# W_in brought in group by group to both halves, and x of the first blocks asked for sooner: a convolution and GELU layer on one Trainium2 core

## Chip, core and metric

The kernel runs on one core of a Trainium2 chip. The metric is the device time of one execution in microseconds (us). Before the change the median of three timed runs is 682.07 us (681.24 to 682.17). The profile is of one execution of 681.4 us; from its first to its last instruction it spans 679.6 us, and all times below are counted from that first instruction.

## What is computed

The input x has 8 sequences of 4,096 tokens with 192 channels. First comes a causal convolution over 7 tokens, whose weights are a softmax for each of 8 heads of 24 channels. Then comes a feed-forward layer with an exact GELU between two matrix products.

```python
w = softmax(weight, axis=-1)                          # 8 heads x 7 taps
x_pad = np.concatenate([np.zeros((B, 6, D)), x], axis=1)
conv = np.einsum('hk,bskhg->bshg', w, unfolded(x_pad)).reshape(B * S, D)
h = conv @ w_in                                       # 192 -> 2048
g = 0.5 * h * (1.0 + erf(h / sqrt(2)))
out = g @ w_out                                       # 2048 -> 192
```

## The kernel before

**Tiling.** The 32,768 tokens are cut into two halves of 16,384. The lower 64 partitions hold the first half, the upper 64 the second. The 192 channels are stored as 3 (`NP`) channels on each of 64 partitions, so a 64-row matmul tile of TensorE serves one half, and the two halves run on different rows of the array. A half is worked through in 35 blocks (`NB`, sizes `WS`): six of 256 tokens, then 29 of 512.

**Slots.** For each block, `mm1` (line 698) makes the 2,048 hidden columns in slots: 8 slots of 256 columns for a block of 256 tokens, 16 slots of 128 for one of 512. ScalarE applies the GELU to a slot's result (line 645), which goes into `gT`; two PSUM buffers `hp` alternate, so slot u waits for the GELU of slot u-2. Between the slots TensorE does shares of `mm2` (lines 742 and 777), the second product, for the block before. For blocks 0 and 1 the convolution is done on TensorE with diagonal weights (`pconv`, line 661); from block 2 on VectorE does it (`conv`, line 495), seven taps on the transposed x.

**W_in on chip.** Both halves need the whole of W_in, so `win` must hold it on partitions 0 to 63 and again on 64 to 127. HBM is read once: GpSimd issues four transfers (`win_in`, line 371), which turn float32 into bfloat16, each to one half of the partitions with two groups of 256 columns: groups 0 and 4 to the lower half, 1 and 5 to the upper, then 2 and 6 to the lower, 3 and 7 to the upper. VectorE copies each to the other half (`dup`, line 459). In its first slots each half uses the groups that came to it directly; the order is the table `CH` (line 86), of which group `ch // 2` and parity `ch % 2` are read in `mm1` and the rows of W_out in `mm2` and `mm2_t`. The first slot waits for two transfers, which share a semaphore, since the halves get theirs by different transfers.

**What sets the order at the start.** GpSimd issues, one after another: three W_in transfers, a part of the diagonal weights (line 397), the fourth, then four of W_out (line 404). SyncE issues x of block 0 and then waits twice: for the fourth small step of the softmax before block 1 (`S_PRO` 4, line 847), and for W_out's third transfer before blocks 2 and 3 (line 849). VectorE runs a list written out by hand (lines 542 to 553): transposes of block 0, its share of `conv_out`, copies of W_in, transposes of block 1, the last copy, `conv_out` of block 1, and then the plan of the blocks from 2. `cast` (line 221) makes the bfloat16 input of `pconv`, on ScalarE for block 0 and on GpSimd for block 1. `mm1` of the first block has its own waits:

```python
if (n, i) == (0, 0):
    t.wait_ge(S_WIN[0], 32)
if n == 0 and i in (4, 6):
    t.wait_ge(S_WIN[i // 2 - 1], 16)
if n == 0 and i in (2, 4, 6):
    t.wait_ge(S_DUPE, 1 + i // 2)
```

## Time and profile before

| what | profile before |
|---|---|
| span | 679.6 us |
| TensorE busy | 674.0 us, 99% |
| ScalarE busy | 537.1 us, 79% |
| VectorE busy | 526.2 us, 77% |
| GpSimd busy | 32.1 us, 5% |
| GELU (line 645), one of 512 | 1.02 us |
| copy within `win` (line 466), one of 4 | 0.56 us |
| W_in, issue to landing | 4.0, 5.5, 6.4 and 7.3 us |
| W_out, issue to landing | 7.1, 7.4, 7.6 and 7.9 us |

The busy time of an engine is the time in which it has an instruction under way. Matmul ends are modelled, so a busy TensorE isn't one at its peak. A row of the profile names a line, an engine, an operation and its tiles (output <- inputs); in square brackets stands how long the engine was idle before it and what ended that. PE is TensorE, PEld its weight loads, DVE VectorE, ACT ScalarE, POOL GpSimd and SP SyncE; a "q" after a name means the engine's own issuing of transfers. Everything that the change touches happens in the first 30 us; the remaining 650 us run in a steady rhythm.

### The profile page before, as it was taken

The page shows a single profiled execution, that of the slowest core. Times are in us where ns is not written, and L with a number is a line of the kernel's source. Part 1 is how long each engine was busy: PE and PEld are TensorE (multiplying, and loading weights), DVE is VectorE, ACT ScalarE, POOL GpSimd, SP SyncE. Part 2 cuts the span into 40 slices and gives each one's busy share as a digit, 9 for nine tenths or more (in the row PEclk, how much of TensorE's full clock was granted, in tenths as well). Part 3 has the DMA queues.
Part 4 walks back from the last instruction along what each step waited for, and adds up shares of the span by engine and source line. Part 5 has one row for each costly group of instructions (what it writes and reads, how often), then busy time and mean ns, then how long its engine had stood idle before and what let it go on. Part 6 is the DMA issues. An engine that isn't in the chain of part 4 may idle for free.

```text
span 679.6 us, 27115 instructions
## 1 busy us (share of the span) xinstructions
PE 674.0 (99%) x12632; PEld 412.8 (61%) x12632; DVE 526.2 (77%) x607; ACT 537.1 (79%) x550; POOL 32.1 (5%) x54
## 2 busy tenths in 40 slices
PE   8999999999999999999999999999999999999998
PEld 7899655555555555555555555555555555555557
DVE  5899978977779877789777798777797777887511
ACT  7899978777778877777877787777878777778772
POOL 5010000000000000000000000000000000000000
DMA  9435324224443234442244432344422344310123
GB/s 147 113 85 140 71 61 93 50 49 96 95 96 79 40 73 96 95 94 51 50 93 95 96 74 51 66 96 95 96 55 50 87 96 95 87 43 16 49 49 96
DMA packets 134145, 53.66 MB, mean 79 GB/s; under 512 B 127376, under 2 KB 134032, under 8 KB 134032
## 3 DMA queue, kind: packets, MB, share of 16 engines
q1 hardware_dynamic: 130224, 49.76, 32.7%
q0 software_dynamic: 2688, 1.57, 1.7%
q8 instruction: 99, 1.62, 1.0%
q10 hardware_dynamic: 1120, 0.59, 0.3%
q14 instruction: 14, 0.11, 0.1%
HBM read 28.31 MB, written 25.17 MB: 79 GB/s over the span
## 4 chain that ended last, share of the span: by engine, by line
PE 95%; DMA 2%; DVE 1%; POOL 0%; SPq 0%; issue 0%; ACT 0%; ACTq 0%
PE hp L732 47%; PE ob L793 43%; PE ob L764 5%; DMA wout<-in_moe_w_out_dram 1%; PE hp L764 1%; DVE acc L521 1%; DMA xin<-in_x_dram 0%; SPq L336 0%; POOL wout L405 0%; DMA wsb<-in_weight_dram 0%; DVE xT L493 0%; DVE wcol L454 0%; DVE xc L521 0%; POOL win L374 0%; POOL dg L397 0%
## 5 line engine op out<-in xcount | busy, mean ns | idle before, releaser
L645 ACT ACTIVATE gT<-hp 128x1024 bf16<-128x1024 f32 x512 | 523.2, 1024 | 128.6 <-PE hp L732 125.3
L732 PE MATMUL hp<-xc,win 64*64 64x512 bf16 (+3 forms) x6072 | 418.6, 365 | 1.8 <-DMA win<-in_moe_w_in_dram 1.1
L793 PE MATMUL ob<-gT,wout 64*64 64x512 bf16 x5376 | 366.3, 376 | 0.0
L521 DVE SCALAR_TENSOR_TENSOR acc<-xT,wcol,acc 128x1024 f32<-128x1024 f32 (+1 forms) x330 | 295.5, 948 | 2.4 <-ACT acc L618 2.4
L732 PEld LDWEIGHTS hp<-xc,win 64*64 64x64 bf16 (+1 forms) x6072 | 188.4, 106 | 134.8 <-ACT xc L200 1.3
L793 PEld LDWEIGHTS ob<-gT,wout 64*64 64x64 bf16 x5376 | 173.4, 118 | 121.8
L323 DVE STREAM_TRANSPOSE osb<-ob 128x512 f32<-128x512 f32 x84 | 74.0, 884 | 129.4 <-PE ob L793 129.4
L493 DVE STREAM_TRANSPOSE xT<-xin 128x1536 f32<-128x1536 f32 (+2 forms) x39 | 74.6, 1920 | 3.3 <-DMA xin<-in_x_dram 3.2
L521 DVE SCALAR_TENSOR_TENSOR xc<-xT,wcol,acc 128x1024 bf16<-128x1024 f32 (+1 forms) x66 | 60.4, 954 | 0.0
L764 PE MATMUL ob<-wout,gT 64*128 64x192 bf16 x896 | 47.5, 243 | 0.1
L423 POOL COPY xT<-xT 128x18 f32<-128x18 f32 x30 | 22.9, 763 | 514.1 <-DVE xT L493 491.9
L764 PEld LDWEIGHTS ob<-wout,gT 64*128 64x128 bf16 x896 | 38.5, 94 | 5.9 <-PE ob L764 0.6
L514 DVE TENSOR_SCALAR acc<-xT,wcol 128x512 f32<-128x512 f32 (+2 forms) x60 | 33.7, 604 | 1.1
L294 ACT ACTIVATE osb<-ob 128x192 f32<-128x192 f32 x2 | 0.7, 331 | 7.1 <-PE ob L764 7.1
L659 PE MATMUL hp<-const-bfloat16-1.0 128*128 128x128 bf16 x48 | 5.3, 310 | 0.8 <-PEq L873 0.8
L764 PE MATMUL hp<-wout,gT 64*128 64x192 bf16 x128 | 5.9, 243 | 0.0
L618 ACT ACTIVATE acc<-xT,wcol 128x256 f32<-128x256 f32 (+1 forms) x9 | 5.2, 580 | 0.5 <-DVE xT L493 0.5
L659 PEld LDWEIGHTS hp<-const-bfloat16-1.0 128*128 128x128 bf16 x48 | 5.0, 145 | 0.8 <-issue 0.8
L292 DVE COPY osb<-ob 128x192 f32<-128x192 f32 x2 | 0.7, 358 | 6.1 <-PE ob L764 6.1
L764 PEld LDWEIGHTS hp<-wout,gT 64*128 64x128 bf16 x128 | 5.3, 94 | 0.0
L279 ACT ACTIVATE osb<-ob 128x384 f32<-128x384 f32 x10 | 4.9, 489 | 0.0
L202 DVE CAST xc<-ob 64x256 bf16<-64x256 f32 (+3 forms) x8 | 2.9, 357 | 2.6 <-PE ob L677 2.4
(35 smaller groups left out, 28.8 us busy)
## 6 DMA issues: line engine op xcount, KB each, us to landing
out_dram<-osb SPq DMA_DIRECT2D x124, 192.0 KB, 3.2
xin<-in_x_dram SPq DMA_DIRECT2D x116, 192.0 KB, 4.0
xin<-in_x_dram SPq DMA_DIRECT2D x22, 96.0 KB, 2.5
win<-in_moe_w_in_dram POOLq DMA_DIRECT2D x4, 192.0 KB, 5.9
wout<-in_moe_w_out_dram POOLq DMA_DIRECT2D x4, 192.0 KB, 7.5
out_dram<-osb ACTq DMA_DIRECT2D x4, 96.0 KB, 1.9
out_dram<-osb SPq DMA_DIRECT2D x4, 96.0 KB, 2.5
xin<-in_x_dram ACTq DMA_DIRECT2D x2, 96.0 KB, 2.5
```

Of the source, the lines that this page charges most:

```text
L279: e.activation(out=dst, in_=src, func=AF.Copy).then_inc(S_EVA)
L323: v.transpose(ap(osb[m % 2], j, [[8 * C, 128], [C // 2, TB // 32], [NP, 32]]), bank(ring(m, j)),).then_inc(S_EV)
L423: g.tensor_copy(dst, src).then_inc(S_HALO)
L493: v.transpose(out, src).then_inc(S_TR)
L514: ins = v.tensor_scalar(a, src, wk, None, ALU.mult)
L521: ins = v.scalar_tensor_tensor(dst, src, wk, a, op0=ALU.mult, op1=ALU.add)
L618: a.activation(out=acc[n % 2][:, p * TB : p * TB + w], in_=ap(xT[n % 2], p * XW + HX, [[NP * XW, 128], [1, w]]), func=AF.Copy, scale=wcol[ ...
L645: a.activation(out=ap(gT[n % 2], i * c * 2 * w, dst), in_=ap(hp[u % 2], 0, src), func=AF.Gelu,).then_inc(S_GELU)
L659: t.matmul(hp[1][:, 0:128], one, one)
L732: ins = t.matmul(hp[u % 2][fo : fo + fw, o : o + w], ap(win, f1, [[NP * F, 64], [2, fw]]), xc[n % 2][r, p * TB : p * TB + w], start=(p == ...
L764: ins = t.matmul(bb[sub], gT[m % 2][r, c0 : c0 + 128], wout[r, CH[sub][i] * C : (CH[sub][i] + 1) * C], start=(ph == 0 and k == 0), stop=(p ...
L793: ins = t.matmul(bank(ring(m, j), slice(64 * h, 64 * h + 64), w), ap(wout, 64 * hf * NF * C + CH[h][i] * C + j, [[NF * C, 64], [NP, 64]],) ...
```

## The change

Each W_in transfer now brings the 256 columns of one group to the lower half and those of the neighbouring group to the upper half at once, in the place of the even group in both. So transfer q serves a slot of both halves by itself, and has a semaphore of its own. The order is groups 0 and 1, 4 and 5, 2 and 3, 6 and 7. `dup` makes two copies for each transfer, of half the size each, from either half into the odd group's place of the other. In the upper half neighbouring groups therefore lie exchanged, which `mm1` undoes with `^ hf`. The slots take own and copied groups in the order own 0, own 1, copied 0, copied 1, own 2, copied 2, own 3, copied 3. The copies come in another order on VectorE. SyncE asks for x of block 1 after the second step of the softmax instead of the fourth, for block 2 after the fourth W_in transfer instead of W_out's third, and for block 3 after W_out's fourth. `mm2` waits for W_out's third and fourth transfers together. The purpose is an earlier first slot and an earlier convolution of block 2.

```diff
-    CH = [
-        [4 * (i // 8) + 2 * ((i // 4 + hf * (i < 8)) % 2) + 8 * (i // 2 % 2) + i % 2 for i in range(NF)]
-        for hf in range(2)
-    ]
+    CG = [[0, 4, 1, 5, 2, 3, 6, 7], [1, 5, 0, 4, 3, 2, 7, 6]]
+    CH = [[2 * CG[hf][i // 2] + i % 2 for i in range(NF)] for hf in range(2)]
...
-        def part(s, hf):
-
-            return FQ * (2 * s + hf), [[NP * F, 64], [4 * FQ, 2 * NP], [1, FQ]]
+        def part(q):
+
+            return FQ * (4 * (q % 2) + 2 * (q // 2))
...
-            def win_in(s, sm, hfs):
-                for hf in hfs:
-                    c0, pat = part(s, hf)
-                    g.dma_start(
-                        ap(win, 64 * hf * NP * F + c0, pat), ap(wint, c0, pat)
-                    ).then_inc(sm[hf], 16)
+            def win_in(q):
+                g.dma_start(
+                    ap(win, part(q), [[NP * F, 128], [F, NP], [1, FQ]]),
+                    ap(wint, part(q), [[FQ, 2], [NP * F, 64], [F, NP], [1, FQ]]),
+                ).then_inc(S_WIN[q], 16)
...
-            def dup(s, hf):
-
-                if s == 0:
-                    v.wait_ge(S_WIN[0], 32)
-                else:
-                    v.wait_ge(S_WIN[1 + hf], 16)
-                c0, pat = part(s, hf)
-                v.tensor_copy(
-                    ap(win, 64 * (1 - hf) * NP * F + c0, pat), ap(win, 64 * hf * NP * F + c0, pat)
-                ).then_inc(S_DUPE)
+            def dup(q):
+
+                v.wait_ge(S_WIN[q], 16)
+                for hf in range(2):
+                    pat = [[NP * F, 64], [F, NP], [1, FQ]]
+                    v.tensor_copy(
+                        ap(win, 64 * (1 - hf) * NP * F + part(q) + FQ, pat),
+                        ap(win, 64 * hf * NP * F + part(q), pat),
+                    ).then_inc(S_DUPE)
...
-            dup(0, 0)
-            dup(0, 1)
-            dup(1, 0)
+            dup(0)
+            dup(1)
             for p in range(NP):
                 trans(1, p)
-            dup(1, 1)
+            dup(2)
+            dup(3)
...
-                if (n, i) == (0, 0):
-                    t.wait_ge(S_WIN[0], 32)
-                if n == 0 and i in (4, 6):
-                    t.wait_ge(S_WIN[i // 2 - 1], 16)
-                if n == 0 and i in (2, 4, 6):
-                    t.wait_ge(S_DUPE, 1 + i // 2)
+                if n == 0:
+                    j = (0, 1, 0, 1, 2, 2, 3, 3)[i]
+                    if i in (0, 1, 4, 6):
+                        t.wait_ge(S_WIN[j], 16)
+                    else:
+                        t.wait_ge(S_DUPE, 2 * j + 2)
...
-                        f0 = 256 * (ch // 2) + ch % 2
+                        f0 = FQ * ((ch // 2) ^ hf) + ch % 2
...
-                        if n < 2 and un[:2] == (0, 0) and un[2] in (0, 8, 12):
-                            for q in {0: (0, 1), 8: (2,), 12: (3,)}[un[2]]:
+                        if n < 2 and un[:2] == (0, 0) and un[2] in (0, 8):
+                            for q in (un[2] // 4, un[2] // 4 + 1):
                                 t.wait_ge(S_WOUT[q], 16)
...
-            sp.wait_ge(S_PRO, 4)
+            sp.wait_ge(S_PRO, 2)
             load(sp, 1)
-            sp.wait_ge(S_WOUT[2], 16)
+            sp.wait_ge(S_WIN[3], 16)
             load(sp, 2)
+            sp.wait_ge(S_WOUT[3], 16)
             load(sp, 3)
```

## The prediction

> **What bounds the kernel now.** I read the page first, then the chain of waits, then the first 30 us in order of time. Row 1 of the page has TensorE (PE) busy for 674.0 of 679.6 us. The chain's answer lists the parts that ended last:

> ```profile
> 7.38 7.64 DMA wout<-in_moe_w_out_dram
> 15.39 1.16 SPq L336
> 17.09 2.61 DMA xin<-in_x_dram
> 19.71 1.24 DVE xT L493
> 21.66 4.38 DVE acc L521 x9
> 27.04 0.67 DVE xc L521
> 27.85 0.92 PE hp L732 x12
> ```

> (Columns: start, length, what.) From 27.85 us on the chain is PE alone, so a change in the start is worth what it moves the first matmul of block 2, and nothing else. Before 27.85 two lines meet there: x of block 2, asked for only when W_out's third transfer has landed, and the slots of blocks 0 and 1. The second has almost no slack. In order of time:

> ```profile
> 6.04 1.74 PE L677 MATMUL ob<-xTb,dg 64*64 64x256 bf16 x56
> 7.04 1.09 ACT L200 ACTIVATE xc<-ob 128x256 bf16<-128x256 f32 x3 [0.63 <-PE ob L677]
> ...
> 8.92 1.49 PE L732 MATMUL hp<-xc,win 64*128 64x256 bf16 x24 [1.14 <-DMA win<-in_moe_w_in_dram]
> 9.79 3.89 ACT L645 ACTIVATE gT<-hp 128x1024 bf16<-128x1024 f32 x4 [1.66 <-PE hp L732]
> ...
> 12.54 0.36 PEld L677 LDWEIGHTS ob<-xTb,dg 64*64 64x64 bf16 x16 [0.21 <-POOL xTb L228]
> ...
> 13.88 5.12 ACT L645 ACTIVATE gT<-hp 128x1024 bf16<-128x1024 f32 x5 [0.20 <-PE hp L732]
> ...
> 27.85 0.92 PE L732 MATMUL hp<-xc,win 64*128 64x256 bf16 x12 [0.16 <-DVE xc L521]
> ```

> The first slot waits 1.14 us for W_in, though the convolution ended at 7.78. From 9.79 to 19.0 the Gelus (1.02 us each) pace the slots; then PE does (1.23 us a slot). So the time at which the first slot starts passes to the end almost undiminished, in either direction.

> **How the transfers land.** Issue (line L374) plus "to landing" of the single W_in transfers gives 2.46+4.0 = 6.5, 3.30+5.5 = 8.8, 3.97+6.4 = 10.4 and 5.25+7.3 = 12.55 us. W_out's land at 13.05, 14.05, 15.0 and 16.05, and the last piece of x of block 1 at 4.75+6.1 = 10.85. Windows of half a microsecond (last two columns: DMA share, GB/s):

> ```profile
> 4.00:4.50 0.50, 0.50 (x7) 0.50 (x6) 0.44 (x3) 0.33 (x2) 0.50 (x1) 1.00 0.74 76
> ...
> 5.00:5.50 0.50, 0.50 (x8) 0.50 (x7) 0.50 (x3) 0.50 (x3) 0.50 (x2) 1.00 1.22 156
> ...
> 13.00:13.50 0.50, 0.50 (x28) 0.50 (x24) 0.19 (x1) 0.50 (x1) 0.25 (x1) 1.00 1.31 201
> ```

> W_in starts to move at 4.0. With all 16 DMA engines at work it moves 156 GB/s, 9.75 per engine; W_out, in longer rows, 201 GB/s, 12.6 per engine.

> [...] The page says

> ```profile
> q1 hardware_dynamic: 130224, 49.76, 32.7%
> q0 software_dynamic: 2688, 1.57, 1.7%
> ```

> SyncE's transfers, counted from the code by rows: x 65,024 and stores 60,928, with 16 closing packets for each of their 138 + 128 transfers 4,256; together 130,208. That leaves 16 for the convolution weights (8 rows, line 844): 8 rows and 8 closing packets. So 8 outer rows ran on 8 engines[...]. For GpSimd's queue q0 the trace can't decide: each of its 8 transfers has an outer count of 64 or 128 on both sides (1,536 + 1,024 rows + 128 closing packets = 2,688). [...] Line 659's 48 matmuls take 5.27 us, 110 ns each[...].

> **The change part by part.**

> *The new transfer.* Its source starts with `[FQ, 2]`, its destination with 128 partitions. [...] Its 384 rows of 512 B are 196,608 B as before; at 9.75 GB/s on each of two engines that is 10.1 us where 16 engines would need 1.3. The bounds: 7.8 us at W_out's 12.6 GB/s; 17.1 us if I take the slow mean of all four W_in transfers beside x (786 KB from 4.0 to 12.55: 5.75 GB/s per engine). On those engines x of block 1 passes too: 393 KB over 16 engines is 24.6 KB, at the 15.8 GB/s per engine of the window from 2 to 3 us (253 GB/s) 1.5 us. I take 4.0 + 10.1 + 1.5 = 15.6 us for the first landing, with 12.3 and 18.5 as likely ends. I assume that the four take different pairs of engines, so that they run side by side: by their issue times the second lands 0.8, the third 1.5, the fourth (less disturbed by x) 1.6 to 2.5 us later.

> *First slot.* It needs one transfer instead of two, a gain of 8.8 - 6.5 = 2.3 us had speeds stayed; of that only the 1.14 us wait could be used. With the landing at 15.6 the first matmul moves from 8.92 to 15.7: +6.8 us.

> *Cold PE.* PE is idle from 7.8 to 15.7[...]. A slot's 12 matmuls take 0.66 us warm (15.14 to 15.81), so 1.3 cold, against the Gelu's 1.02. The first slot loses 0.65 and each further cold one 0.3[...]; up to 2.5 if the cold stretch takes in the convolution of block 1 (16 matmuls, 0.47 us warm). I take 1.4.

> *Later slots.* Second slot: its transfer lands before PE is done with the first. Third and fourth: their copies follow on VectorE at once. A copy of 768 elements lies between 0.28 (half of the 555 ns row) and 0.56 us[...]. Behind the waiting copies VectorE has queued block 1's transposes and conv_out; they move from 10.96 to about 17 us, by as much as the slots, and x has long landed. So the 0.20 us stall at 13.88 (casts of block 1) goes: -0.2.

> *x of blocks 1 and 2.* Block 1 is asked for 0.45 us sooner (3.02 instead of 3.47). Block 2 waits for the fourth W_in transfer, about 17.2, instead of W_out's third at 15.0; queued behind it on SyncE are only block 3 and stores that begin at 25.9. It lands 4.65 us after the issue as now (15.03 to 19.69): 21.9, and its convolution ends at 28.0+2.2 = 30.2. PE comes to block 2 about 7.5 us later than now, at 35: the stall of some 0.33 us (26.29 to 27.85 against 1.23) goes: -0.3.

> *W_out.* Queued behind W_in on the engines, one transfer per microsecond from about 17.2: landed at 18 to 21. First use moves to about 23.5, that of the third and fourth to 25.5: no wait. Other edits rename slots and cost nothing: same matmuls, weights and order.

> Sum: 6.8 + 1.4 - 0.2 - 0.3 = +7.7; 682.07 + 7.7 = 689.8 us.

> **Rivals.** *A (forecast), two engines, side by side: 0.82.* [...] Ends: 12.3 + 0.1 - 8.92 = 3.5, +0.5 cold, -0.5 stalls: 685.6; 18.5: 9.7 + 2.5 - 0.5 = 11.7: 693.8.
> *B, 16 engines after all[...]: 0.09.* The first slot then starts at 7.9, when ScalarE's second conv_out ends (7.83), 1.0 sooner; the 0.2 and 0.33 stalls go, less what a late x of block 1 gives back (next case): about -1.2, 680.9, with -1.6 at best. For it: the waits shown. [...]
> *C, 16 engines, but x of block 1 holds the gain: 0.06.* It lands some 0.4 sooner at best, so the casts of block 1 let the fifth Gelu start only 0.4 sooner, and with a part of the 0.33 the sum is -0.6: 681.5, no change.
> *D, two engines, the same for all four: 0.03.* The fourth lands at about 4 + 4 x 10.1 + 1.5 = 46 instead of about 20.5 when it is due (15.14 + 7 less the stalls): over 20 us slower, some 710.

> The range, 684.5 to 694.5, takes in A with its bounds and leaves out B, C, D and A's tails, 2 in 10. Slower: A and D, 0.85; within 0.2% (1.36 us): C and a part of B, 0.08; faster: the rest, 0.07.

> **What would show it.** In the changed profile: first W_in landing near 15.6 instead of 6.5 us; a PE wait of about 8 us for W_in ahead of the first slot; DMA moving far under 150 GB/s from 6 to 15 us; the first Gelu near 17; slots of over 1.1 us just after; no idle ahead of block 2 near 35; steady state unchanged. Wrong at once if the first transfer lands by 8 us: then B or C, told apart by whether the casts of block 1 still hold the fifth Gelu. If a copy or W_out ends PE's wait later, the hidden parts were mis-sized.

## The result, and the profile after

The changed kernel takes 691.8 us (median of 4 runs, 690.99 to 692.33); the kernel before takes 681.68 us in the same comparison. The ratio is 1.0147, with a 95% interval from 1.013 to 1.0165: 10.1 us slower. The forecast was 689.8 us, 684.5 to 694.5.

The profiled execution is the longest of the four; its span is 690.5 us against 679.6. From block 2 on both kernels do the same in the same rhythm: from its first matmul to the end it takes 651.6 us, and 651.7 before. So the difference lies in the first 40 us. The chain of waits of the changed kernel (start, length, what):

```profile
2.45 2.63 POOL win L370
5.08 13.99 DMA win<-in_moe_w_in_dram
19.12 4.04 PE hp L728 x36
```

The chain no longer passes through W_out, x of block 2 and VectorE. It goes through GpSimd's first W_in issue, then the second W_in transfer, which lands at 19.1 us, and from there through PE to the end. The same stretch in order of time:

```profile
2.45 7.59 POOL L370 DMA_DIRECT2D win<-in_moe_w_in_dram  x3 [0.62 <-DMA wsb<-in_weight_dram]
...
3.21 1.84 DVE L442 TENSOR_SCALAR wnm<-wex,wrc 8x7 f32<-8x7 f32 x1
...
10.11 0.61 POOL L394 TENSOR_TENSOR dg<-idb,wcol 128x256 bf16<-128x256 bf16 x1
...
10.87 3.19 PE L673 MATMUL ob<-xTb,dg 64*64 64x256 bf16 x56 [5.43 <-POOL dg L394]
...
16.05 0.83 PE L728 MATMUL hp<-xc,win 64*128 64x256 bf16 x12 [1.99 <-DMA win<-in_moe_w_in_dram]
...
16.92 1.02 ACT L641 ACTIVATE gT<-hp 128x1024 bf16<-128x1024 f32 x1 [3.23 <-PE hp L728]
...
19.12 4.04 PE L728 MATMUL hp<-xc,win 64*128 64x256 bf16 x36 [2.24 <-DMA win<-in_moe_w_in_dram]
...
25.31 5.12 ACT L641 ACTIVATE gT<-hp 128x1024 bf16<-128x1024 f32 x5 [1.09 <-PE hp L728]
...
38.89 0.82 PE L728 MATMUL hp<-xc,win 64*128 64x256 bf16 x12
```

The first slot starts at 16.05 us instead of 8.92, and PE waits another 2.24 us for W_in ahead of the second. GpSimd needs 7.59 us for three issues that took 2.15. The page's row for GpSimd's queue shows what grew with it (queue, packets, MB, share of 16 engines):

```profile
q0 software_dynamic: 13440, 1.62, 2.6%
```

There were 2,688 packets before. The surplus of 10,752 is 4 x 14 x 192. All of it is in packets under 512 B (by the page 138,128 in all queues, 127,376 before), and the bytes hardly grow (1.57 to 1.62 MB). This number comes out if, for each of the four transfers, two of the 16 engines carry the 384 rows (192 each) and each of the other 14 gets as many small fillers. No view shows the engines one by one, so "two engines" is here and below a reading of the count, to be tested. The windows view, with the granted PE clock third from the end, then DMA share and GB/s:

```profile
7.00:8.00 1.00, 0.00 (x0) 0.00 (x0) 0.57 (x2) 1.00 (x4) 1.00 (x2) 0.94 0.48 18
8.00:10.00 2.00, 0.00 (x0) 0.00 (x0) 0.00 (x0) 0.02 (x1) 2.00 (x1) 0.50 0.61 30
10.00:12.00 2.00, 1.13 (x22) 1.12 (x26) 0.00 (x0) 0.00 (x0) 1.93 (x3) 0.50 0.69 44
12.00:14.00 2.00, 2.00 (x42) 1.79 (x34) 0.42 (x1) 1.03 (x3) 2.00 (x3) 0.50 0.76 63
...
16.00:18.00 2.00, 0.83 (x12) 0.58 (x12) 0.78 (x2) 1.02 (x1) 0.29 (x2) 1.00 1.20 106
18.00:20.00 2.00, 0.88 (x10) 0.63 (x12) 0.84 (x3) 0.00 (x0) 0.00 (x0) 0.53 1.47 148
20.00:22.00 2.00, 2.00 (x22) 1.24 (x20) 1.32 (x3) 1.12 (x2) 1.34 (x4) 0.50 1.22 132
```

Between x of block 1, landed at 7.1 us, and W_out, first issued at 13.2, W_in has the engines nearly to itself. It moves at 18 GB/s with one transfer issued (7 to 8 us), 30 with two (8 to 10) and 44 with three (10 to 12): the rate grows with the number of transfers under way. It would do so if each has its own pair of engines, which no view shows. The 156 GB/s of before were not W_in alone, since x of block 1 was under way there until 10.85 us. The clock granted to PE is at half from 7.9 to 14.7 us and again from 18.1 to 24.9.

**Where 11.0 us went.** Block 2's first matmul moves from 27.85 to 38.89 us, +11.04. The first slot is 7.13 later. From the first Gelu to the fifth it takes 8.39 us (16.92 to 25.31) instead of 4.09: +4.30, of which 2.24 is the second slot's wait. The other 2.06 should be the half clock. From the fifth Gelu to block 2 it takes 13.58 instead of 13.97: -0.39. The sum, 7.13 + 2.24 + 2.06 - 0.39, is 11.04.

### The profile page after: what moved, and what is told of

The parts are those of the page before. It is cut to its first block, busy times and chain, and to the rows that moved or that the text cites. A ratio compares the mean times of both kernels' runs of the same rounds, so it can differ in the third digit from the quotient of the medians.

```text
span 690.5 us, 27122 instructions
## 1 busy us (share of the span) xinstructions
PE 677.1 (98%) x12632; PEld 413.3 (60%) x12632; DVE 528.9 (77%) x611; ACT 536.8 (78%) x550; POOL 38.6 (6%) x54
## 2 busy tenths in 40 slices
DMA packets 144897, 53.70 MB, mean 78 GB/s; under 512 B 138128, under 2 KB 144784, under 8 KB 144784
## 3 DMA queue, kind: packets, MB, share of 16 engines
q1 hardware_dynamic: 130224, 49.76, 32.1%
q0 software_dynamic: 13440, 1.62, 2.6%
q8 instruction: 99, 1.62, 1.0%
## 4 chain that ended last, share of the span: by engine, by line
PE 97%; DMA 2%; POOL 0%; issue 0%; DVE 0%
PE hp L728 48%; PE ob L789 42%; PE ob L760 5%; DMA win<-in_moe_w_in_dram 2%; PE hp L760 1%; POOL win L370 0%; PE ob L673 0%; DMA wsb<-in_weight_dram 0%; DVE osb L290 0%
## 5 line engine op out<-in xcount | busy, mean ns | idle before, releaser
L673 PE MATMUL ob<-xTb,dg 64*64 64x256 bf16 (+1 forms) x112 | 5.3, 323 | 5.4 <-POOL dg L394 5.4
L370 POOL DMA_DIRECT2D win<-in_moe_w_in_dram x4 | 10.1, 2525 | 0.6 <-DMA wsb<-in_weight_dram 0.6
L200 DVE CAST xc<-ob 64x256 bf16<-64x256 f32 (+3 forms) x8 | 2.9, 357 | 7.2 <-PE ob L673 7.1
L673 PEld LDWEIGHTS ob<-xTb,dg 64*64 64x64 bf16 x112 | 4.4, 138 | 6.1 <-issue 6.0
L461 DVE COPY win<-win 64x768 bf16<-64x768 bf16 x8 | 3.4, 420 | 5.6 <-DMA win<-in_moe_w_in_dram 5.4
```

The source lines that it names most:

```text
L370: g.dma_start(ap(win, part(q), [[NP * F, 128], [F, NP], [1, FQ]]), ap(wint, part(q), [[FQ, 2], [NP * F, 64], [F, NP], [1, FQ]]),).then_inc ...
L673: ins = t.matmul(bank(kd, slice(64 * ho, 64 * ho + 64), w), dg[r, d0 : d0 + 64], xTb[PC[n]][r, x0 : x0 + w], start=(k == KS - 1), stop=(k ...
```

## The experiments

The theory is that two outermost rows of the source put each transfer on two engines, and that this alone costs the time. The rivals are that slot order, split copies or SyncE's new waits cost it, or that 2 is a special case.

### The change with W_in in two transfers for each group

```diff
-    g.dma_start(ap(win, part(q), [[NP * F, 128], [F, NP], [1, FQ]]),
-        ap(wint, part(q), [[FQ, 2], [NP * F, 64], [F, NP], [1, FQ]])).then_inc(S_WIN[q], 16)
+    for hf in range(2):
+        pat = [[NP * F, 64], [F, NP], [1, FQ]]
+        g.dma_start(ap(win, 64 * hf * NP * F + part(q), pat),
+            ap(wint, part(q) + hf * FQ, pat)).then_inc(S_WIN[q], 16)
...
-    wait_ge(S_WIN[q], 16)
+    wait_ge(S_WIN[q], 32)      # on PE, VectorE and SyncE
```

> The changed kernel with each of the four W_in transfers issued as two, one for each half of the partitions (64 rows of the source outermost instead of 2), all else as in the change. Theory (the transfers ran on 2 engines): the loss goes; first transfer pair lands by 7 us, first slot starts near 7.9 us, and the time is 680.9, at most 681.7. Rival (slot order, split copies or the new waits of SyncE cost the time): it stays above 688. Rival C of the prediction: 681.5 with the fifth Gelu still held by the casts of block 1.

Measured: 681.7 us, ratio to before 1.0005 (0.9997 to 1.0014). The whole loss is gone with the split copies, the slot order and SyncE's waits still in place, so those cost nothing net. But nothing is gained either. The page and the order of time of this kernel:

```profile
q0 software_dynamic: 2752, 1.57, 1.7%
```

```profile
6.41 0.61 POOL L396 TENSOR_TENSOR dg<-idb,wcol 128x256 bf16<-128x256 bf16 x1
...
7.17 1.74 PE L675 MATMUL ob<-xTb,dg 64*64 64x256 bf16 x56 [1.08 <-POOL dg L396]
...
8.99 1.49 PE L730 MATMUL hp<-xc,win 64*128 64x256 bf16 x24
9.27 2.60 DVE L463 COPY win<-win 64x768 bf16<-64x768 bf16 x4
...
12.95 0.11 PEld L675 LDWEIGHTS ob<-xTb,dg 64*64 64x64 bf16 x2 [0.39 <-POOL xTb L226]
...
14.69 5.12 ACT L643 ACTIVATE gT<-hp 128x1024 bf16<-128x1024 f32 x5 [0.78 <-PE hp L730]
```

The wait for W_in ahead of the first slot is gone, yet that slot starts at 8.99 as in the kernel before: the diagonal weights are now made behind six issues instead of three (6.41 us instead of 4.69), and the convolution starts 1.1 us later. The fifth Gelu is later than before (14.69 against 13.88): four copies take 2.6 us ahead of block 1's transposes, whose casts then hold PE. The outcome is rival C's, but not its reason. C had x of block 1 landing late; here it had landed by 9.1 us (4.4 + 4.7), and the transposes began only at 11.90, when the copies were done.

### Two, four and eight outermost rows, with nothing else changed

In the kernel before, only the source pattern of W_in is exchanged, for the same count and size of rows. These three kernels therefore work with other columns of W_in than the layer needs.

```diff
-    ap(wint, c0, pat)
+    ap(wint, c0, [[2 * FQ, 2], [F, 192], [1, FQ]])        # 2
+    ap(wint, c0, [[2 * FQ, 4], [2 * F, 96], [1, FQ]])     # 4
+    ap(wint, c0, [[FQ, 8], [4 * F, 48], [1, FQ]])         # 8
```

> The kernel before with one thing changed: the source of each W_in transfer is read as 2 x 192 rows (two outermost), same number and size of rows and same destination, so wrong columns reach W_in on chip. Theory: two outer rows alone put the transfers on 2 engines, GpSimd's issue goes from 0.7 to about 2.5 us each, q0's packets grow by 4 x 2,688, first slot (which needs two transfers) starts near 19.2 us, time +10 to +13: 692 to 695. Rival (the rest of the change costs): 681.7.

> The kernel before with the source of each W_in transfer read as 4 x 96 rows (4 outermost), same count and size of rows, so wrong columns reach W_in on chip. Theory (the outer count sets the engines, and GpSimd writes a closing-sized filler for each row on each engine left out): 4 x (12 x 96) = 4,608 more packets on its queue, 7,296; issue about 1.2 us; two transfers landed near 11.7; first slot 2.8 us later and 684 to 686. Rival (2 is special, 4 as 16): 2,688 packets and 681.4.

> The same with 8 x 48 rows (8 outermost), wrong columns too. Theory: 4 x (8 x 48) = 1,536 more packets, 4,224; issue 0.85 us; first slot within 0.7 us of before; 681.4 to 682.6. Rival: 2,688 packets and 681.4.

| outermost | packets of q0 | one W_in issue | first slot at | time | runs |
|---|---|---|---|---|---|
| 64 (before) | 2,688 | 0.66 to 0.84 us | 8.92 us | 681.4 to 681.9 us | 20 to 33 |
| 8 | 4,224 | 0.83 to 1.05 us | 10.56 us | 684.27 us | 1 |
| 4 | 7,296 | 1.18 to 1.36 us | 13.81 us | 686.77 us | 1 |
| 2 | 13,440 | 1.79 to 1.99 us | 19.16 us | 692.95 us | 4 |

The packet rows of the three pages, for 2, 4 and 8 in turn:

```profile
q0 software_dynamic: 13440, 1.62, 2.7%
```

```profile
q0 software_dynamic: 7296, 1.59, 2.1%
```

```profile
q0 software_dynamic: 4224, 1.58, 1.8%
```

All three counts were forecast to the packet. They come out if as many engines work as there are outermost rows and each engine left out gets a filler for each row of a working one: 4 x 14 x 192, 4 x 12 x 96 and 4 x 8 x 48 over 2,688. The counts are measured, the share of the engines is the reading of them. With 2 the ratio to before is 1.0167 (1.0153 to 1.0181): the source pattern alone reproduces the loss. It is even a little above the change's 1.0147; here the first slot still needs two transfers, and PE waits longer in one piece:

```profile
19.16 4.69 PE L733 MATMUL hp<-xc,win 64*128 64x256 bf16 x48 [7.12 <-DMA win<-in_moe_w_in_dram]
```

One issue with 2 outermost rows was forecast at 2.5 us and took 1.8 to 2.0. The losses with 4 and 8 were forecast too small: for 8 the time was expected at 682.6 at most. There is only one run of each, but the first slots (13.81 with 4 and 10.56 with 8) are also plainly later than forecast, 11.7 and at most 9.6.

### Only the first transfer with two outermost rows

```diff
     def win_in(q):
+        if q == 0:
+            (as in the change)
+            return
+        for hf in range(2):
+            (64 partitions each, as in the first experiment)
```

> The changed kernel with only the first W_in transfer left as in the change (2 outermost); the other three issued as two of 64 partitions each. Theory (the second slot's 2.24 us wait comes from the 2.5 us issues and the 2-engine transfers behind the first): first slot still near 16 us, second slot with no wait of over 0.3, W_out landed by 20 us; PE partly cold; 688.4 with a warm clock, 690 with a cold one, so 1.5 to 3 under the change. Rival (the first landing is all of the loss): as the change, 691.5.

Measured: 689.02 us, ratio 1.0104 (1.0088 to 1.0119), 2.8 us under the change.

```profile
q0 software_dynamic: 5424, 1.58, 1.9%
```

```profile
16.28 5.32 PE L736 MATMUL hp<-xc,win 64*128 64x256 bf16 x48 [4.35 <-DMA win<-in_moe_w_in_dram]
```

```profile
18.00:20.00 2.00, 2.00 (x22) 1.20 (x18) 1.91 (x6) 1.74 (x2) 1.27 (x4) 0.50 0.17 25
20.00:22.00 2.00, 2.00 (x28) 1.14 (x28) 1.21 (x3) 1.46 (x3) 0.30 (x2) 0.50 0.80 177
```

The packet count again fits the reading, for the one transfer: 2,688 of before, 48 for three transfers more (the 64 of the first experiment for four), and 14 x 192 fillers. The first slot is as late as in the change (16.28), and the second follows without a wait. So the 2.24 us wait comes from the issues and transfers behind the first one, as assumed. The clock is at half here too, from 15.2 to 22.0 us, and the first five Gelus start 1.28 to 1.43 us apart instead of about 1.02.

### The clock kept up

Matmuls with no use stand ahead of the first and the second slot of the changed kernel.

```diff
+    if n == 0 and i < 2:
+        for _ in range((16, 34)[i]):
+            t.matmul(hp[1][:, 0:128], one, one)
     if n == 0:
         j = (0, 1, 0, 1, 2, 2, 3, 3)[i]
```

> The changed kernel with idle matmuls (128 columns, result unused) ahead of the first slot (16) and the second (34), where PE waits for W_in. Theory: the clock stays up from 16 to 25 us, the cold cost of about 2.1 us goes (second slot 0.5, up to the fifth Gelu 1.6): 689.7. Rival (the halved clock costs nothing, ScalarE paces anyway): 691.8.

Measured: 692.03 us, ratio 1.0153 (1.0136 to 1.017): no gain that the times show. The order of time says more:

```profile
17.00 1.02 ACT L641 ACTIVATE gT<-hp 128x1024 bf16<-128x1024 f32 x1 [3.32 <-PE hp L731]
...
23.34 3.16 ACT L641 ACTIVATE gT<-hp 128x1024 bf16<-128x1024 f32 x3 [0.51 <-PE hp L731]
...
26.00 0.51 PE L763 MATMUL ob<-wout,gT 64*128 64x192 bf16 x8 [0.56 <-DMA wout<-in_moe_w_out_dram]
```

```profile
18.00:20.00 2.00, 2.00 (x38) 1.79 (x37) 1.21 (x3) 0.16 (x2) 0.00 (x0) 1.00 1.45 149
20.00:22.00 2.00, 1.53 (x34) 0.99 (x32) 0.97 (x3) 1.99 (x3) 1.34 (x4) 1.00 1.20 131
```

The clock is at 1.00 from 18 to 22 us, and the first to the fifth Gelu take 6.34 us instead of 8.39: the 2.05 us expected of the clock are there. Then PE waits for W_out's second transfer (landed at 25.8), and the profiled span, 689.3 us, is only 1.2 us shorter than the change's. So the half clock slows these slots by 2 us, but it isn't a cost of its own in full: without it PE waits for W_out, which GpSimd issues from 13.16 us on, after its last W_in issue (10.66 to 13.16). That the remaining 1.2 us are a gain is not shown. The timed runs, 691.05 to 693.23, show none of it, and the profiled execution is the fastest of the four here and was the slowest of the four there.

### x sooner, alone

```diff
-    sp.wait_ge(S_PRO, 4)
+    sp.wait_ge(S_PRO, 2)
     load(sp, 1)
-    sp.wait_ge(S_WOUT[2], 16)
+    sp.wait_ge(S_WIN[2], 16)
     load(sp, 2)
+    sp.wait_ge(S_WOUT[3], 16)
     load(sp, 3)
```

> The kernel before with SyncE's new waits alone: block 1 after the softmax's second step, block 2 after the last W_in transfer, block 3 after W_out's fourth. Theory: only the 0.33 us stall ahead of block 2 and part of the 0.2 us stall of the fifth Gelu go: -0.3 to -0.5, 681.3. Rival: x beside W_in delays it, no gain or a loss of up to 0.5.

Measured: 681.17 us, ratio 0.9996 (0.9988 to 1.0005): no difference that can be measured.

```profile
9.75 1.49 PE L732 MATMUL hp<-xc,win 64*128 64x256 bf16 x24 [1.61 <-DMA win<-in_moe_w_in_dram]
...
14.76 5.13 ACT L645 ACTIVATE gT<-hp 128x1024 bf16<-128x1024 f32 x5 [0.25 <-PE hp L732]
```

In the profiled execution, which at 681.76 us lies above the median, the first slot starts 0.83 us later than before (9.75 against 8.92). W_in's second transfer lands at 9.7 instead of 8.8 us, and of the three waits only that of block 1 can have acted by then: x of block 1 is under way beside W_in sooner. From the fifth Gelu to block 2 it takes 13.65 us instead of 13.97. So what is won ahead of block 2 is lost ahead of block 0.

### The change repaired

These are three kernels, all with W_in in two transfers of 64 partitions for each group. In the first (`e5_dg_between` in the expectations) the diagonal weights are made after two groups instead of three. The second is the first with x of block 1 asked for as in the kernel before. The third is the first with block 1's convolution placed one slot later; "the last" in its expectation means the first kernel.

```diff
-    for q in range(3):
+    for q in range(2):
         win_in(q)
     g.wait_ge(S_PRO, 9)
     (diagonal weights)
+    win_in(2)
     win_in(3)
...
-    sp.wait_ge(S_PRO, 2)                 # second kernel
+    sp.wait_ge(S_PRO, 4)
...
-    behind = {(0, 3): p01[:8], (0, 4): p01[8:] + p2[:2], (0, 5): p2[2:]}    # third
+    behind = {(0, 4): p01[:8], (0, 5): p01[8:] + p2[:2], (0, 6): p2[2:]}
```

> As the changed kernel with each W_in transfer issued as two of 64 partitions, and the diagonal weights on GpSimd made after two groups (four issues) instead of three (six). Theory (the gain was lost since GpSimd made the diagonal weights 1.7 us later, behind six issues): the convolution starts near 6.1 us instead of 7.17, the first slot near 7.9, and the time is 680.4 to 681.0, 0.4 to 1.0 under before. Rival (the copies on VectorE ahead of block 1's transposes hold the fifth Gelu near 13.9 whatever the first slot does): first slot at 7.9 but no more than 0.4 gained, 681.1.

> As e5_dg_between with x of block 1 asked for as in the kernel before (after the softmax's fourth step). Theory (x of block 1 asked for sooner shares the engines with W_in, so the second slot waits 0.84 us for its W_in): that wait falls under 0.4 and the time to about 680.3, 0.4 under e5. Rival (x of block 1 then lands later and its casts hold the fifth Gelu): 680.7 or up to 681.2.

> As the last, with block 1's convolution on TensorE placed behind slots 4, 5 and 6 of block 0 instead of 3, 4 and 5. Theory (it is block 1's casts that hold the fifth Gelu): that wait goes, fifth Gelu near 12.8, block 2 at about 26.4 and 680.1, 1.3 under before. Rival (then block 1's first slot waits for its own conv_out): as the last kernel, within 0.3.

Measured, as ratios to before: 0.9985 (0.9978 to 0.9991), 680.71 us, for the first; 0.9983 (0.9976 to 0.999), 680.48 us, for the second; 0.9993 (0.9985 to 1.0002), 681.31 us, for the third. The first:

```profile
7.83 0.83 PE L731 MATMUL hp<-xc,win 64*128 64x256 bf16 x12 [0.16 <-ACT xc L198]
...
9.50 1.49 PE L731 MATMUL hp<-xc,win 64*128 64x256 bf16 x24 [0.84 <-DMA win<-in_moe_w_in_dram]
...
12.21 0.36 PEld L676 LDWEIGHTS ob<-xTb,dg 64*64 64x64 bf16 x16 [0.21 <-POOL xTb L226]
...
13.55 5.12 ACT L644 ACTIVATE gT<-hp 128x1024 bf16<-128x1024 f32 x5 [0.20 <-PE hp L731]
```

Now the change does what it was for: the first slot starts 1.09 us sooner than before, with no wait for W_in. The fifth Gelu is only 0.33 sooner; a wait of 0.84 us for W_in ahead of the second slot and the casts of block 1 have taken the rest. In the second kernel that wait falls to 0.35 us, as forecast, but the fifth Gelu is hardly sooner (13.51), and the 0.4 us forecast did not come: the two times can't be told apart.

```profile
9.08 1.60 PE L731 MATMUL hp<-xc,win 64*128 64x256 bf16 x24 [0.35 <-DMA win<-in_moe_w_in_dram]
```

The third brought no gain where 1.3 us were forecast:

```profile
10.89 6.15 ACT L644 ACTIVATE gT<-hp 128x1024 bf16<-128x1024 f32 x6 [0.45 <-PE hp L731]
...
16.78 0.51 PE L763 MATMUL ob<-wout,gT 64*128 64x192 bf16 x8 [0.35 <-DVE xc L200]
```

The wait ahead of the fifth Gelu is indeed gone: the second to the seventh follow one another. But PE then waits for block 1's own conv_out ahead of `mm2`, much as the rival had it, and the kernel is 0.6 us slower than the first. The first two kernels are some 0.15% faster than the kernel before, and so faster than the changed one too.

## Why the prediction was right, and where its terms were off

The direction was right, and so was its place: the loss goes with the source pattern and comes with it (681.7 us without it in the change, 692.95 with it alone). That two outermost rows mean two engines was my estimate. What the page before gave for it was one transfer of SyncE, with 8 rows and 8 further packets where the others have 16. The packet counts for 2, 4 and 8 (13,440, 7,296 and 4,224) agree with it exactly, but no view shows an engine at work. 689.8 us was 2.0 us short of the 691.8 measured, and that it came so near is in part luck. Step by step, by the profile:

- *First landing, 15.6 us forecast, 15.95 found* (2.45 + 13.5): two errors that cancel. I let the transfer start at 4.0 us as before, but its issue ends only at 5.08 instead of 3.30. I added 1.5 us for x of block 1 on the same engines, but that had landed by 7.1 us (4.4 + 2.7). The 10.1 us for the transfer itself rested on 156 GB/s for W_in, from a window in which x of block 1 had its part, so this speed had not been seen for W_in alone; the transfer took about as long, 10.9 us from the end of its issue. That the four run side by side was right. First slot: +6.8 forecast, +7.13 found.
- *Second landing*: this is the step that failed. I had it 0.8 us after the first, "by their issue times" of the kernel before, and so no wait. It lands 3.1 us after the first (5.08 + 14.0 = 19.1), mostly because an issue takes 2.5 us instead of 0.7. The missing term is 2.24 us; leaving only the first transfer with two outermost rows removes it.
- *Cold PE*: 1.4 us forecast, 2.06 by the difference of the Gelus and 2.05 with the clock kept up. That the wait would halve the clock, and for how long, was my estimate; what a half costs is shown: at a granted 0.50 the 36 matmuls from 19.12 us on took 4.04 us (112 ns each), while at 1.00, in the run with the clock kept up, 24 of them took 1.49 (62 ns). The stretch took in the convolution of block 1, the case that I had bounded at 2.5. The clock was not low from the first slot on, as I had it. The first slot, at 16.05, ran at 1.00: the granted clock had risen at 14.71, shortly after the convolution of block 0, itself delayed to 10.87 us; it fell again at 18.12, in the wait ahead of the second slot.
- *Stalls that go*: -0.5 forecast, -0.39 found between the fifth Gelu and block 2. But the stall ahead of the fifth Gelu did not go: it is 1.09 us, from the cold PE, which the term above holds.
- *Hidden parts*: x of block 2 was forecast to land at 21.9 us and its convolution to end at 30.2, well ahead of PE. It landed only at 30.4, since SyncE asks for it after the fourth W_in transfer (23.8); VectorE waited 2.53 us for it (line below), and the convolution ended at 38.8, just ahead of block 2's first matmul at 38.89. PE shows no wait there, but the margin that I had counted on is gone. W_out was forecast at 18 to 21 us; it landed at 24.8 to 27.7 (issues at 13.2 to 15.4 plus 11.6 to 12.3). The first two transfers, in by 26.0, are still ahead of their use at 27.2, and PE shows no wait for the others, but there is far less to spare, as the run with the clock kept up shows. A copy takes 0.42 us in the mean, between the 0.28 and 0.56 that I had put as bounds; the eight are 3.4 us.

```profile
30.45 1.22 DVE L489 STREAM_TRANSPOSE xT<-xin 128x768 f32<-128x768 f32 x1 [2.53 <-DMA xin<-in_x_dram]
```

- *Not foreseen*: GpSimd's long issues delay the diagonal weights to 10.11 us and the convolution to 10.87. It cost nothing, because W_in came later still; in the first experiment, with six issues ahead of the weights, it took most of the gain: with four ahead the kernel is 1.0 us faster (680.71 against 681.7).

The sum of the found terms, 7.13 + 2.24 + 2.06 - 0.39, exceeds the forecast 7.7 by 3.3 in the profiled execution, the longest of the four; in the medians the excess over the forecast difference is 10.1 - 7.7 = 2.4.

Rivals B and C could be looked at all the same, in the kernel of the first experiment, whose 2,752 packets show no surplus but 16 for each of four transfers more. B's 680.9 did not come about there (681.7). C's outcome did, no change with the fifth Gelu held by block 1's casts, but it was the copies on VectorE and not x of block 1 that made the casts late.

## What to carry to other kernels

Before a transfer is made to serve more partitions at once, look at the outermost count of its source, not only at its bytes: here a leading 2 in the source cost 10.1 us, where two transfers with 64 rows outermost moved the same data without loss (681.7 us). Count the packets of GpSimd's queue on the page: 13,440 instead of 2,688 was the sign here. And when GpSimd issues transfers and also computes, an added issue delays what stands behind it: the diagonal weights began at 4.69 us behind three issues, at 5.16 behind four and at 6.41 behind six. So a needed computation belongs between the issues, where its input comes ready.

## What the runs showed of the hardware that was not expected

- A GpSimd transfer with fewer outermost rows in its source isn't only slower to land (5.9 us after its issue in the median with 64, 7.2 with 8, 9.6 with 4, 15.0 with 2) but slower to issue. With 64 partitions as destination the issue took 0.66 to 0.84 us with 64 outermost rows, 0.83 to 1.05 with 8, 1.18 to 1.36 with 4 and 1.79 to 1.99 with 2; with 128 partitions and 2 outermost rows it took 2.5 to 2.6.
- A VectorE step of the softmax (8 x 7 elements) that began during the first issue took 1.84 us in the changed kernel instead of 0.22, and ended at 5.05 against 5.08 for the issue. With 2, 4 and 8 outermost it took 1.19, 0.55 and 0.25 us; with 2 it ended at 4.37 against 4.41. That the issue holds the step up is not shown: no run here took GpSimd out of the way alone.
- A copy of 768 elements too took 0.71 us in the first experiment while GpSimd issued W_out, and 0.42 in the changed kernel, where GpSimd's last issue ended 0.14 us after the copy began. That the issue is the reason is not shown:

```profile
9.27 0.71 DVE L463 COPY win<-win 64x768 bf16<-64x768 bf16 x1
```

```profile
15.94 0.42 DVE L461 COPY win<-win 64x768 bf16<-64x768 bf16 x1 [1.55 <-DMA win<-in_moe_w_in_dram]
```

```profile
14.50:15.00 0.50, 0.00 (x0) 0.00 (x0) 0.00 (x0) 0.00 (x0) 0.50 (x2) 0.79 0.91 78
...
18.00:18.50 0.50, 0.00 (x0) 0.00 (x0) 0.00 (x0) 0.00 (x0) 0.00 (x0) 0.62 1.21 149
```

  A mean of 0.79 over half a microsecond is 0.21 us at half and 0.29 at full clock, so the rise is at 14.71. With only the first transfer on two outermost rows the means of 0.58, 0.56 and 0.79 (8 to 10, 10 to 12 and 14 to 16 us) and the 0.50 up to 22 put the changes at 8.3, 11.8, 15.2 and 22.0 us, the same distances apart to within the tenth. In the changed kernel, after a stretch with 0.83 us of matmuls (14.71 to 18.12) the clock fell, after 2.4 (18.12 to 21.53) it stayed at half, and after 2.8 (11.29 to 14.71) and 3.4 (21.53 to 24.95) it rose. PE had been idle for only 1.2 us when the clock fell at 18.12. In the first microseconds, ahead of the first change that it shows, the column stands at 1.00, although the matmuls there took 110 ns each (line 659 of the kernel before). In the run with the clock kept up matmuls of the same shape took 118 ns at a granted 0.50 (16 in 1.89 us) and 64 at 1.00 (34 in 2.17).
